# A third buffer for raw and converted weight words, in the place of three attention tiles that are first used from the second batch on

## The chip, the cores and the metric

The kernel runs on one core of a Trainium2 chip. The metric is the time of one launch in device microseconds (us): the median of several runs, 1111.56 us before the change (3 runs, 1110.79 to 1111.98). One further run was taken with the hardware profiler; it took 1109.59 us, and its trace spans 1107.8 us from the first to the last instruction.

## What is computed

Attention with a per-position decay (4 batches, 8 heads, 576 positions, head size 64), then two feed-forward layers over the 2304 tokens that come out of it. The weights arrive as float64.

```
def _attn_ref(q, k, v, f):
    scores = scale * np.matmul(q, k.transpose(0, 1, 3, 2))
    log_f = np.log(np.clip(f, 0.0001, 1.0))
    cum = np.cumsum(log_f, axis=-1)
    decay = cum[:, :, :, None] - cum[:, :, None, :]
    scores = np.where(causal, -1000000000.0, scores + decay)
    attn = softmax(scores)
    return np.matmul(attn, v)

def reference(...):
    x = attn_out as [2304, 512]
    h = x @ moe_w_in                      # 512 -> 2048
    x = np.maximum(0.01 * h, h) @ moe_w_out
    return ((x @ w_a) * (x @ w_b)) @ w_o2  # 512 -> 1536 -> 512
```

## The kernel before, in words

One program interleaves attention and the first feed-forward layer; the second layer follows. A list scheduler decides each engine's order when the program is built, so the order of the source is a priority and not the final order. On the chip every engine then works its own list strictly in order, and so does each queue that issues DMAs (SP issues nearly all of them).

**Attention** is cut into (batch, r): r = 0 is the first 256 queries of a batch, r = 1 the other 320. `att_scores` (L170) makes a head's scores, adds the decay, takes the row's extreme and the exponential; `att_values` (L377) transposes the weights, multiplies them with v and writes its part of a token chunk `xh`, `xl` (a high and a low part whose sum is the f32 value). Batch 0 loads q and k in rows and transposes them on TensorE in f32; from batch 1 on they are transposed on VectorE into tiles `tq` and `tk`, and `qll` holds the low part of q. So `tq`, `tk` and `qll` are first used in batch 1, with one exception: `ones` (L144), at the start, shares the space of `tk`.

**The first layer** works on chunks of 256 tokens: `l1` (L563) multiplies with w_in, 24 matmuls of 128x256 for a pair of feature blocks, `l2` (L591) with w_out. Products take three passes: high by high, low by high, high by low.

**The weights.** 16 blocks of w_in (`wi_0` to `wi_15`) and 16 of w_out (`wo_0` ...) are loaded in the order wi_0, wo_0, wi_1, wo_1, ... by `load_weight` (L105): a DMA of 512 KB brings float64 words into a tile `raw`; ScalarE takes an absolute value of the top words into a tile `c` (L94); VectorE clamps, shifts and merges in four instructions (L95, L96, L97, L100); `split` (L85) then copies the high part on ScalarE (L87) and subtracts on VectorE for the low part (L88, tiles `wi_lo`, `wo_lo`). `raw` and `c` have two buffers each, in the pool `stage`:

```
raw = stg_pool.tile([P, W, 2], I32, tag="raw", bufs=RB, name=f"raw_{name}_{z}")
...
c = stg_pool.tile([P, W], I32, tag="t", bufs=2, name=f"c_{name}_{z}")
```

So the DMA of a block waits until L100 of the block two places ahead of it has read its words. The conversions are interleaved with the attention of batch 0 on VectorE. The main part (after L742) runs `att_steps(0)` with `load_next` every ninth step, then `att_steps(1)` with `load_next` every eighth and a `work` item (an `l1` and the `l2` before it) every sixteenth, then the remaining items of chunk 0, four items of chunk 1, closes `stage` (L769) and goes on with batch 1.

## Time and profile before

| | |
|---|---|
| median of 3 runs | 1111.56 us (1110.79 to 1111.98) |
| the profiled execution's own time | 1109.59 us |
| span of its trace | 1107.8 us |
| TensorE (PE) busy | 97% of the span |
| VectorE (DVE) busy | 55% |
| ScalarE (ACT) busy | 49% |
| GpSimd (POOL) busy | 18% |
| mean traffic of the DMA engines | 78 GB/s |

Busy shares are means over stages that have different limits; the attention of batch 0 with the weights fills the first 166 us or so, and the last 400 us are matmuls almost alone. The granted clock is that of TensorE, 1.00 for 2.4 GHz and 0.50 for 1.2 GHz. Matmuls are pipelined and their ends are modelled in the trace, so how densely they are packed is better read from their starts than from the busy share.

### The profile page before, as it was taken

Reading aid. Unit: us, or ns where it says so; the run is one execution under the profiler, and the core shown is the slowest. Engines: PE = TensorE matmul, PEld = TensorE weight load, DVE = VectorE, ACT = ScalarE, POOL = GpSimd, SP = SyncE. Lnnn points to the kernel's source line nnn. Section 1 sums busy time; section 2 is a strip of 40 time slices with the busy share of each in tenths; the row PEclk is TensorE's granted clock in tenths of the full one; section 3 lists DMA queues with packets and bytes.
Section 4 is the critical chain, followed back from the end, with each engine's and each line's share of the span. In section 5 each row is a group of like instructions: output and inputs, shape, how many; then the busy total and the mean of one; then the engine's idle time right before and its main releaser. Section 6 shows DMA issues by size and latency. Waiting matters only on the chain.

```text
span 1107.8 us, 19615 instructions
## 1 busy us (share of the span) xinstructions
PE 1079.2 (97%) x7021; PEld 967.2 (87%) x7021; DVE 614.0 (55%) x1484; ACT 543.2 (49%) x1257; POOL 204.5 (18%) x434
## 2 busy tenths in 40 slices
PE   5899999999999999999999999999999999999998
PEld 3577779999999999999999997888888888888897
DVE  5869887887777777677478877412111211211122
ACT  4656668878787878768554454312111211211121
POOL 4423322434243432333000000102001000100000
PEclk9879999999999999999999999999999999999999
DMA  7645545442452334422054454202000100100010
GB/s 196 195 130 172 159 120 103 96 94 48 79 124 62 94 58 83 109 62 53 9 165 144 142 152 152 76 1 76 1 1 20 48 1 1 48 1 1 1 39 20
DMA packets 185729, 86.77 MB, mean 78 GB/s; under 512 B 143840, under 2 KB 173536, under 8 KB 185632
## 3 DMA queue, kind: packets, MB, share of 16 engines
q1 hardware_dynamic: 180736, 80.80, 28.6%
q10 hardware_dynamic: 4896, 4.72, 1.3%
q8 instruction: 56, 0.92, 0.4%
q14 instruction: 41, 0.34, 0.1%
HBM read 75.96 MB, written 9.51 MB: 77 GB/s over the span
## 4 chain that ended last, share of the span: by engine, by line
PE 72%; DMA 11%; DVE 8%; ACT 4%; issue 3%; SPq 1%; POOL 0%; ACTq 0%; DVEq 0%; POOLq 0%
PE ab L653 25%; PE o L676 13%; PE h L574 11%; PE y L601 10%; PE s L76 5%; PE av L76 5%; PE pp L76 3%; DMA raw_wa<-in_moe_w_a_dram 3%; DMA raw_wb<-in_moe_w_b_dram 2%; DMA raw_wc<-in_moe_w_out_dram 1%; DMA xq<-in_q_dram 1%; DMA cumb<-cum_dram 1%; DMA raw_wi<-in_moe_w_in_dram 1%; DMA raw_wo<-in_moe_w_out_dram 1%; DMA sy<-y_dram 1%
## 5 line engine op out<-in xcount | busy, mean ns | idle before, releaser
L659 DVE TENSOR_TENSOR p<-ab,p 128x512 f32<-128x512 f32 (+1 forms) x60 | 38.3, 638 | 274.6 <-PE ab L653 272.0
L574 PE MATMUL h<-xh,wi_hi 128*128 128x256 f32 x576 | 164.6, 286 | 1.2 <-ACT wi_hi L87 1.2
L574 PE MATMUL h<-xh,wi_lo 128*128 128x256 f32 x576 | 164.1, 285 | 0.9 <-DVE wi_lo L88 0.9
L574 PE MATMUL h<-xl,wi_hi 128*128 128x256 f32 x576 | 164.3, 285 | 0.0
L601 PE MATMUL y<-gl,wo_hi 128*128 128x256 f32 x576 | 161.7, 282 | 1.0 <-DVE gl L586 1.0
L601 PE MATMUL y<-gh,wo_lo 128*128 128x256 f32 x576 | 161.1, 282 | 0.0
L601 PE MATMUL y<-gh,wo_hi 128*128 128x256 f32 x576 | 159.4, 282 | 0.0
L658 ACT COPY p<-ab 128x512 f32<-128x512 f32 (+1 forms) x60 | 32.7, 544 | 169.1 <-PE ab L653 168.7
L574 PEld LDWEIGHTS h<-xh,wi_hi 128*128 128x128 f32 x576 | 109.8, 191 | 5.2 <-issue 2.3
L574 PEld LDWEIGHTS h<-xh,wi_lo 128*128 128x128 f32 x576 | 109.8, 191 | 2.5 <-DVE wi_lo L88 1.1
L601 PEld LDWEIGHTS y<-gl,wo_hi 128*128 128x128 f32 x576 | 108.4, 188 | 2.9 <-DVE gl L586 1.6
L574 PEld LDWEIGHTS h<-xl,wi_hi 128*128 128x128 f32 x576 | 109.8, 191 | 0.8 <-issue 0.4
L601 PEld LDWEIGHTS y<-gh,wo_lo 128*128 128x128 f32 x576 | 108.3, 188 | 1.7 <-issue 1.2
L601 PEld LDWEIGHTS y<-gh,wo_hi 128*128 128x128 f32 x576 | 107.3, 188 | 1.8 <-issue 0.8
L313 POOL TENSOR_SCALAR p<-cumb,ncum_t 128x384 f32<-128x384 f32 (+1 forms) x112 | 75.1, 678 | 162.4 <-PE pp L76 47.8
L87 ACT CAST pph<-p 128x512 fp32r<-128x512 f32 (+1 forms) x60 | 34.8, 580 | 126.3 <-DVE p L659 126.2
L291 ACT ACTIVATE p<-p,stat 128x384 f32<-128x384 f32 (+4 forms) x128 | 77.0, 603 | 34.5 <-DVE stat L320 27.2
L88 POOL TENSOR_TENSOR yl<-sy,yh 128x512 fp32r<-128x512 f32 (+1 forms) x16 | 19.2, 1211 | 393.7 <-ACT yh L87 393.6
L653 PE MATMUL ab<-yh,wb_hi 128*128 128x512 f32 (+1 forms) x240 | 88.3, 368 | 0.9 <-DVE p L659 0.6
L653 PE MATMUL ab<-yh,wa_hi 128*128 128x512 f32 (+1 forms) x240 | 88.1, 367 | 0.0
L653 PE MATMUL ab<-yh,wa_lo 128*128 128x512 f32 (+1 forms) x240 | 88.1, 367 | 0.0
L653 PE MATMUL ab<-yl,wa_hi 128*128 128x512 f32 (+1 forms) x240 | 88.1, 367 | 0.0
(168 smaller groups left out, 2612.6 us busy)
## 6 DMA issues: line engine op xcount, KB each, us to landing
cumb<-cum_dram SPq DMA_DIRECT2D x32, 288.0 KB, 3.9
raw_wi<-in_moe_w_in_dram SPq DMA_DIRECT2D x16, 512.0 KB, 4.0
raw_wo<-in_moe_w_out_dram SPq DMA_DIRECT2D x16, 512.0 KB, 4.0
raw_wa<-in_moe_w_a_dram SPq DMA_DIRECT2D x12, 512.0 KB, 3.5
raw_wb<-in_moe_w_b_dram SPq DMA_DIRECT2D x12, 512.0 KB, 3.5
raw_wc<-in_moe_w_out_dram SPq DMA_DIRECT2D x12, 512.0 KB, 3.6
xq<-in_q_dram SPq DMA_DIRECT2D x144, 32.0 KB, 2.0
y_dram<-yo ACTq DMA_DIRECT2D x18, 256.0 KB, 3.0
```

Of the source, the lines that this page charges most:

```text
L76: return method(*args, **kw)
L87: nc.scalar.copy(hi, src)
L88: (lo_engine or nc.gpsimd).tensor_tensor(out=lo, in0=src, in1=f32(hi), op=ALU.subtract)
L291: act_att.activation(pt, pt, AF.Exp, bias=stat[:, 0, s : s + 1], scale=-1.0, accum_out=stat[:, 1, s : s + 1])
L313: pool_att.tensor_scalar(pt, cumb[:, :n], 1.0, ncum_t[:, t, bh : bh + 1], op0=ALU.mult, op1=ALU.add)
L574: nc.tensor.matmul(hps[:, u, :], w[:, c * P : c * P + P], x[:, c, :], start=(n == 0), stop=(n == 3 * ND - 1))
L601: nc.tensor.matmul(o, w[:, d * P : d * P + P], g[:, u, :], start=(fi == 0 and n == 0 and d % 2 == 0), stop=(fi == NF1 - 1 and n == 2 and d ...
L653: nc.tensor.matmul(o[:, :tn], w[:, c * P : c * P + P], y[:, c, :tn], start=(m == 0), stop=(m == 3 * ND - 1))
L658: nc.scalar.copy(p[:, :tn], ab[0][:, :tn])
L659: nc.vector.tensor_tensor(out=p[:, :tn], in0=ab[1][:, :tn], in1=p[:, :tn], op=ALU.mult)
L676: nc.tensor.matmul(o, g[:, t * P : t * P + P], w, start=(fi == 0 and m == 0), stop=(fi == NF2 - 1 and m == 2))
```

## The change

Every third weight block (counted by `piece`: wi_1, wo_2, wi_4, wo_5, ..., wo_14, ten in all) takes its `raw` and its `c` from a new pool `more` with one buffer of each, as long as that pool is open. `more` lies in the attention part of the memory. It is closed when `stage` is, before batch 1 of attention, and a new pool `att_b` then takes its place, with `tq`, `qll` (two buffers) and `tk`. `ones` goes to the space of `p4`. Nothing else changes in what is computed.

```
         for z in range(0, 512, W):
-            raw = stg_pool.tile([P, W, 2], I32, tag="raw", bufs=RB, name=f"raw_{name}_{z}")
+            third = "more" in late and piece[0] % 3 == 2
+            piece[0] += 1
+            words, bufs = (late["more"], 1) if third else (stg_pool, RB)
+            raw = words.tile([P, W, 2], I32, tag="raw", bufs=bufs, name=f"raw_{name}_{z}")
...
-            c = stg_pool.tile([P, W], I32, tag="t", bufs=2, name=f"c_{name}_{z}")
+            c = words.tile([P, W], I32, tag="t", bufs=1 if third else 2, name=f"c_{name}_{z}")
...
-    late = {}
+    late, piece = {}, [0]
...
+    more_ctx = att_ctx.enter_context(ExitStack())
+    late["more"] = more_ctx.enter_context(tc.tile_pool(name="more", bufs=1))
...
-    ones = ap_.tile([B * H, S], F32, tag="tk", name="ones")
+    ones = ap_.tile([B * H, S], F32, tag="p4", name="ones")
...
-            tq = ap_.tile([P, 320], F32, tag="tq", name=f"tq_{nm}")
+            tq = late["att"].tile([P, 320], F32, tag="tq", name=f"tq_{nm}")
...
-            qll = ap_.tile([P, 384], F32R, tag="qll", bufs=2, name=f"qll_{nm}")
+            qll = late["att"].tile([P, 384], F32R, tag="qll", bufs=2, name=f"qll_{nm}")
...
-                tk = ap_.tile([P, S], F32, tag="tk", name=f"tk_{nm}")
+                tk = late["att"].tile([P, S], F32, tag="tk", name=f"tk_{nm}")
...
     stage_ctx.close()
+    more_ctx.close()
+    del late["more"]
+    late["att"] = more_ctx.enter_context(tc.tile_pool(name="att_b", bufs=1))
```

The change moves instructions on every engine, since the scheduler sees other waits. (Line numbers in the changed kernel are 3 to 8 higher. In the names, `_0_0_7` is batch 0, r = 0, head 7; the last number is a running one.) Three places:

**SP's queue at the start.** `cumb` are the decay rows for the first heads, `xq` and `xk` queries and keys, `vn` values. Before:

```order
L392 DMA vn_0_0_0_209<-in_v_dram 128x2x64
L392 DMA vn_0_0_2_321<-in_v_dram 128x2x64
L283 DMA cumb_0_0_0_121<-cum_dram_58 128x256 x2
L283 DMA cumb_0_0_2_158<-cum_dram_58 128x256 x2
L194 DMA xq_0_0_4_229<-in_q_dram 128x2x64 x2
L283 DMA cumb_0_0_4_242<-cum_dram_58 128x256
L197 DMA xk_0_0_4_230<-in_k_dram 128x2x64 x2
L283 DMA cumb_0_0_4_242<-cum_dram_58 128x256
L114 DMA raw_wi_1_0_262<-in_moe_w_in_dram 128x4x256
L116 DMA raw_wo_1_0_274<-in_moe_w_out_dram 128x1024
```

With the change:

```order
L397 DMA vn_0_0_0_212<-in_v_dram 128x2x64
L117 DMA raw_wi_1_0_265<-in_moe_w_in_dram 128x4x256
L288 DMA cumb_0_0_0_124<-cum_dram_58 128x256 x2
L288 DMA cumb_0_0_2_161<-cum_dram_58 128x256 x2
L199 DMA xq_0_0_4_232<-in_q_dram 128x2x64 x2
L288 DMA cumb_0_0_4_245<-cum_dram_58 128x256
L202 DMA xk_0_0_4_233<-in_k_dram 128x2x64 x2
L288 DMA cumb_0_0_4_245<-cum_dram_58 128x256
L119 DMA raw_wo_1_0_277<-in_moe_w_out_dram 128x1024
```

The words of wi_1 are now asked for ahead of the decay rows and of the queries and keys of head 4; before they came behind them.

**TensorE (PE) just ahead of the first layer's first matmul** (`h_0_0`; `px` is the transposed output of the last pair of heads of r = 0, the `s`, `s4`, `pp`, `tq`, `tk` rows are attention of r = 1). Before:

```order
L76 MATMUL px_0_0_7_614<-ident_65,xn_0_0_7_587 128x128 x2
L76 MATMUL s4_0_1_0_0_760<-kn_0_1_0_709,qn_0_1_0_708 64x288
L76 MATMUL pp_0_1_0_0_807<-ident_65,p_0_1_0_2_736 128x128 x3
L76 MATMUL s4_0_1_0_1_763<-kn_0_1_0_709,qn_0_1_0_708 64x288
L76 MATMUL pp_0_1_0_1_813<-ident_65,p_0_1_0_3_745 128x128 x4
L76 MATMUL tq_0_1_2_935<-ident_65,xq_0_1_2_925 128x128 x2
L76 MATMUL tq_0_1_2_935<-ident_65,xk_0_1_2_926 128x64
L76 MATMUL tk_0_1_2_0_940<-ident_65,xk_0_1_2_926 128x128 x2
L76 MATMUL s_0_1_1_2_803<-kn_0_1_0_709,qn_0_1_0_708 128x384
L574 MATMUL h_0_0_619<-xh_0_309,wi_0_hi_185 128x256
```

With the change:

```order
L76 MATMUL px_0_0_7_617<-ident_65,xn_0_0_7_590 128x128 x2
L76 MATMUL s_0_1_1_2_806<-kn_0_1_0_712,qn_0_1_0_711 128x384
L76 MATMUL tk_0_1_2_0_943<-ident_65,xk_0_1_2_929 128x128 x2
L76 MATMUL tk_0_1_2_2_947<-ident_65,xk_0_1_2_929 128x128 x2
L76 MATMUL tk_0_1_2_2_947<-ident_65,xk_0_1_2_929 128x64
L76 MATMUL s_0_1_1_3_827<-kn_0_1_0_712,qn_0_1_0_711 128x512
L579 MATMUL h_0_0_622<-xh_0_312,wi_0_hi_188 128x256
```

Four items of r = 1 (`s4` and `pp`, twice each) now stand ahead of `px`, and three more transposes `tk_0_1_2_2` and one more score `s_0_1_1_3` ahead of `h_0_0`. On VectorE the same stretch holds more conversions: of its 160 conversion instructions (L95, L96, L97, L100 and L88 of 32 blocks), 52 stood ahead of the fourth `xl` (the one that reads this `px`), and 71 stand there now: 15, 15, 14, 14 and 13 of the five lines for 11, 11, 10, 10 and 10 before.

**VectorE (DVE) where the conversions end.** Before, words of the last two blocks are converted between instructions of batch 1:

```order
L320 ISA p_1_0_1_1_2265,stat_1_0_0_2176<-s_1_0_1_1_2270,p_1_0_1_1_2265 128x256
L320 ISA stat_1_0_0_2176 128x1
L97 SCALAR_TENSOR_TENSOR c_wo_15_0_1617<-raw_wo_15_0_1615,c_wo_15_0_1617 128x512
L239 STREAM_TRANSPOSE tq_1_0_3_2363<-xq_1_0_3_2358 128x256
L297 RECIPROCAL rec_1_0_0_0_2220<-rec_1_0_0_0_2220 128x2
L270 TENSOR_TENSOR ks_1_0_4_2440<-tk_1_0_4_2438,ks_1_0_4_2440 64x256
L296 TENSOR_SCALAR rec_1_0_1_2_2283<-stat_1_0_0_2176 128x2
L100 SCALAR_TENSOR_TENSOR c_wo_15_0_1617<-raw_wo_15_0_1615,c_wo_15_0_1617 128x512
L297 RECIPROCAL rec_1_0_1_2_2283<-rec_1_0_1_2_2283 128x2
L586 TENSOR_TENSOR gl_0_7_1847<-hs_0_7_1845,gh_0_7_1846 128x512
```

With the change:

```order
L88 TENSOR_TENSOR wo_14_lo_1479<-c_wo_14_0_1482,wo_14_hi_1478 128x512
L96 TENSOR_SCALAR c_wo_15_0_1620<-c_wo_15_0_1620 128x512
L366 ISA p4_0_1_4_1388,stat_0_1_4_1224<-s4_0_1_5_1_1568,p4_0_1_4_1388,st4_0_1_5_1560 64x288
L366 ISA stat_0_1_4_1224 64x1
L244 STREAM_TRANSPOSE tq_1_0_0_2189<-xq_1_0_0_2184 128x256
L268 STREAM_TRANSPOSE tk_1_0_0_2200<-xk_1_0_0_2195 128x256
L88 TENSOR_TENSOR wi_15_lo_1605<-c_wi_15_0_1608,wi_15_hi_1604 128x512
L97 SCALAR_TENSOR_TENSOR c_wo_15_0_1620<-raw_wo_15_0_1618,c_wo_15_0_1620 128x512
```

The first transpose of batch 1, `tq_1_0_0`, follows 156 of the 160 conversion instructions, where it followed 126 before; it cannot stand ahead of those of wo_14, the last block in `more`, whose memory it takes. The last block is now done while heads 5 and 6 of batch 0 are at work.

## Rows read from the trace of the kernel before

**Rows 1.** Busy time, share of the span and instructions of each engine

```profile
PE 1079.2 (97%) x7021; PEld 967.2 (87%) x7021; DVE 614.0 (55%) x1484; ACT 543.2 (49%) x1257; POOL 204.5 (18%) x434
```

**Rows 2.** Stretches: length, busy us (instructions) of each engine, granted clock, DMA share, GB/s

```profile
5.00:10.00 5.00, 2.37 (x13) 1.34 (x11) 2.37 (x6) 2.23 (x6) 0.00 (x0) 1.00 0.98 290
53.60:67.20 13.60, 13.58 (x42) 7.89 (x41) 8.56 (x22) 6.30 (x15) 3.10 (x4) 0.50 0.62 166
69.90:158.00 88.10, 87.26 (x597) 70.22 (x597) 76.97 (x183) 55.20 (x124) 30.53 (x46) 1.00 0.57 158
158.00:162.80 4.80, 2.55 (x20) 2.06 (x18) 4.71 (x17) 2.90 (x8) 0.00 (x0) 1.00 0.18 31
162.80:166.30 3.50, 3.50 (x17) 3.46 (x18) 3.44 (x15) 2.43 (x8) 0.00 (x0) 0.51 0.20 32
166.30:170.00 3.70, 3.70 (x31) 3.46 (x29) 1.94 (x6) 3.65 (x11) 0.00 (x0) 1.00 0.28 46
```

**Rows 3.** Waits of DVE, 0 to 166 us: total us, times, longest

```profile
DVE c_wi L95 <- ACT c_wi L94: 9.7, 9, 2.3
DVE p L320 <- PE s L76: 5.7, 2, 2.9
DVE c_wo L95 <- ACT c_wo L94: 5.2, 5, 2.0
```

**Rows 4.** Waits of DVE, 0 to 58 us

```profile
DVE c_wi L95 <- ACT c_wi L94: 6.3, 6, 2.3
DVE p L76 <- POOL p L76: 2.1, 3, 1.0
...
DVE p L76 <- PE s L76: 1.2, 1, 1.2
DVE c_wo L95 <- ACT c_wo L94: 1.0, 1, 1.0
```

**Rows 5.** Waits of SP's queue, 0 to 166 us

```profile
SPq L116 <- DVE c_wo L100: 28.5, 11, 5.5
SPq L114 <- DVE c_wi L100: 18.0, 10, 2.9
```

**Rows 6.** Timeline of PE, 159.4 to 163.1 us: start, us, what, idle before and its releaser

```profile
159.67 0.27 PE L76 MATMUL s<-ks,qll 128*128 128x128 f32 x1
161.10 0.39 PE L574 MATMUL h<-xh,wi_hi 128*128 128x256 f32 x1 [1.15 <-ACT wi_hi L87]
...
162.76 0.50 PE L574 MATMUL h<-xh,wi_lo 128*128 128x256 f32 x1 [0.92 <-DVE wi_lo L88]
```

**Rows 7.** Groups of DVE by line, 0 to 166 us: busy, mean ns

```profile
L97 DVE SCALAR_TENSOR_TENSOR c_wo<-raw_wo,c_wo 128x512 int32<-128x512 int32 x16 | 12.5, 778 | 0.2
...
L88 DVE TENSOR_TENSOR wi_lo<-c_wi,wi_hi 128x512 fp32r<-128x512 f32 x16 | 11.4, 711 | 0.2
...
L100 DVE SCALAR_TENSOR_TENSOR c_wi<-raw_wi,c_wi 128x512 int32<-128x512 int32 x16 | 11.2, 700 | 0.1
...
L96 DVE TENSOR_SCALAR c_wi<-c_wi 128x512 int32<-128x512 int32 x16 | 7.6, 476 | 0.2
L95 DVE TENSOR_SCALAR c_wo<-c_wo 128x512 f32<-128x512 f32 x16 | 7.5, 466 | 5.2 <-ACT c_wo L94 5.2
```

**Rows 8.** Timeline of DVE, 57.5 to 58.5 us

```profile
57.97 0.41 DVE L76 TENSOR_TENSOR xl<-px,xh 128x256 fp32r<-128x256 f32 x1
```

**Rows 9.** Timeline of PE, 54.9 to 69.9 us

```profile
54.98 0.69 PE L76 MATMUL px<-ident,xn 128*128 128x128 f32 x2
...
60.59 0.69 PE L76 MATMUL tk<-ident,xk 128*128 128x128 f32 x2
61.21 1.65 PE L76 MATMUL s<-kn,qn 64*128 64x384 f32 x2
62.78 0.58 PE L574 MATMUL h<-xh,wi_hi 128*128 128x256 f32 x1
...
67.82 1.12 PE L76 MATMUL s<-kn,qn 64*128 64x512 f32 x2
68.88 0.65 PE L76 MATMUL tk<-ident,xk 128*128 128x128 f32 x3
69.25 0.75 PE L76 MATMUL s<-kn,qn 64*128 64x288 f32 x2
```

**Rows 10.** The chain that ended last, around 190 and 240 us: start, us, what

```profile
189.75 3.59 DMA cumb<-cum_dram
193.51 1.01 POOL p L337
...
239.17 1.07 DVE pl L374 x2
240.29 1.03 PE av L76 x7
```

## The prediction, made before the change was run

> **What bounds the kernel now.** I read first the shares of the whole span [rows 1]: PE is busy for 97%, so a change can save only what PE loses, about 29 us in all plus what it loses to a low clock. Then the stretches [rows 2]. From 69.9 to 158 us, where the weights are still being converted, PE is busy for 87.26 of 88.1 us: it idles 0.84 us there, though the weights are late the whole time. From 158 to 162.8 us it is busy for only 2.55 of 4.80 us, and in the next 3.5 us its granted clock is 0.51, the 1.2 GHz level, with 1.00, 2.4 GHz, on either side. The stretch from 53.6 to 67.2 us also runs at 0.50.
>
> Next the waits. VectorE does wait for weights: 9.7 us before the first instruction of a wi block and 5.2 us before that of a wo block, 14.9 us in all [rows 3]; the releaser named is ScalarE's absolute value, which itself waits for the DMA. SP shows why: the DMAs of weight words waited 28.5 and 18.0 us for L100 to free a buffer [rows 5]. That is the wait which a third buffer loosens. But PE feels little of it: the trace has two waits of PE for a weight in the whole fill, 1.15 us for the high and 0.92 us for the low part of a late w_in block, at 161.10 and 162.76 us [rows 6]. So I price the change by PE's losses, not by VectorE's 14.9 us.
>
> **The change part by part.**
>
> *The end of the fill (a gain).* In the new order the last block is converted while heads 5 and 6 of batch 0 are at work, and no longer between instructions of batch 1. The two waits of PE, 1.15 + 0.92 = 2.07 us [rows 6], should go. What is left of the 2.25 us idle is 0.18 us, for attention. After them PE starts only 17 matmuls in 3.5 us at half clock, against 31 in 3.7 us right behind [rows 2]. Without the hole the clock should stay up, which gives at most half of the stretch, 1.75 us, and at least nothing (if another hole appears); I take 1.5, near the upper end, since PE went into that stretch from 88 us at full clock. Together **-3.6 us**, bounds -3.8 and 0.
>
> *The start (what the front-loading costs).* VectorE works its list in order. Ahead of the fourth `xl`, which completes chunk 0, stand 71 conversion instructions for 52: 4 more of L95, 4 of L96, 4 of L97, 4 of L100, 3 of L88. At 0.47, 0.48, 0.78, 0.70 and 0.71 us [rows 7] that is 4 x 2.43 + 3 x 0.71 = 11.9 us; instructions overlap a little, so say 10 to 11.9. Against this stand VectorE's waits for weights up to 58 us, 6.3 + 1.0 = 7.3 us, which the third buffer can take away, and 2.1 + 1.2 = 3.3 us in which it waited for GpSimd and PE with nothing else to do [rows 4] and where in the new order the conversion of wi_1 stands. So `xl` comes between 10 - 7.3 - 3.3 = 0.6 us earlier and 11.9 - 7.3 = 4.6 us later than the 57.97 us of [rows 8]; I take 1.5 us later, nearer the lower end because those 3.3 us lie exactly where the new work was put. In SP's queue the words of wi_1 move ahead of the first decay rows. The DMA engines are already at 0.98 there and move 290 GB/s [rows 2]; 512 KB at that rate take 1.8 us. That is the upper bound, nothing the lower (the transfers overlap with what nobody waits for yet); I take 0.9. Sum: 2.4 us later on VectorE.
>
> The Trainium skill, "DMA: Bandwidth & Descriptors", section "Issuing engines are not separate DMA queues", says that all DMAs run on the same 16 engines and interleave, whoever issues them. It speaks against asking for weights this early; by it the whole 1.8 us would be paid, and the sum below would be 0.9 us higher.
>
> On PE, `px` (54.98 us) would start at 57.4 us. Behind it now stand `px` itself (0.62 us, by the starts), a score of 384 columns (1.57), two transposes (0.62), three more `tk` (0.37 at full clock, 0.74 at half) and a score of 512 columns (1.06, or 2.12): 5.7 us, so the first `h` starts at 63.1 us for 62.78 us, 0.3 us later. But the last two items, which ran from 67.82 to 69.25 us, 1.43 us of full-clock work, are then already done [rows 9]. Net **-1.1 us**. Bounds: with the lower ends -0.6 - 1.43 = -2.0; with the upper ones 4.6 + 1.8 - 1.43 = +5.0.
>
> *Between 70 and 158 us (nothing, or a little).* PE is packed; its work does not change, and weights that come earlier cannot run on a full engine. The new interleave is another list, and it may hold small holes of its own. The old one cost 0.84 us here; I add the same once more, **+0.8 us**, bounds 0 and 3 (VectorE idles 88.10 - 76.97 = 11.1 us in this stretch, so it has room, but each attention step now queues behind more conversions).
>
> *Edits at no cost.* `ones` in the space of `p4`: it is read once, by the scan at the start, and `p4` is first written in r = 1, long after. `tq`, `tk`, `qll` in `att_b`: the first `tq` has to follow the words of wo_14. Before it stood behind 126 conversions, now behind 156; the cover is that VectorE has lost its 14.9 us of waits by then, which pay for those 30 (30 x 0.63 = 18.9 us) but for 4 us. Should the cover be gone, batch 1 starts 4 us later, the second rival. The last 900 us run the same instructions; PE is simply earlier there.
>
> Sum: -3.6 - 1.1 + 0.8 = **-3.9 us**. Against the profiled execution's own 1109.59 us that is 1105.7 us; that execution was 1.97 us under the median of the runs, so against the median, 1111.56 us, it is **1107.7 us**, 0.35% faster. About 0.2%, 2.2 us, is what a measurement of this kernel can tell from no change.
>
> **The rivals.**
>
> *1. VectorE's bubbles are the bound, and all 14.9 us come off:* 1111.56 - 14.9 = 1096.7 us. For it: VectorE is busy for 76.97 of 88.1 us, and the waits are regular. Against it: PE is packed over the same stretch [rows 2], and a full engine can't follow. Chance 0.05. The Trainium skill, "Perfetto Trace Analysis", section "Optimization Strategy", reads gaps that repeat on the engine that should be saturated as a lack of buffers for the next tile; by it, taken for VectorE, this rival would be the forecast. In this trace the engine that should be saturated is PE, and it has no such gaps.
>
> *2. Batch 1 becomes what PE waits for (no change).* The chain that ended last leaves PE at about 189.75 us, runs over decay rows, GpSimd and VectorE for 50 us and returns to PE at 240.29 us [rows 10]: the attention of batch 1 is just in time now. If PE gets there 4 us earlier and batch 1 does not, PE waits there and the 3.9 us are given back: 1111.6 us. For it: the bound on `tq` above. Against it: with no conversions left VectorE and ScalarE have less between batch 1's steps. That the third buffer frees nothing, since the loads stand in SP's queue behind others, would look the same. Chance 0.22, with the small holes of the new interleave in it.
>
> *3. The start is slower than the end gains (slower).* If VectorE's waits for GpSimd and PE don't absorb anything and the decay rows are late by the full 1.8 us, the first layer starts 5.0 us late net of the work moved ahead. The clock rose only 4.4 us after the first `h` [rows 2, 9], so the half-clock stretch would grow by about the same 5 us, which costs half of that again, 2.5 us. With the gain at the end: +5.0 + 2.5 - 3.6 = +3.9 us, 1115.5 us. It decides from a net delay of about 4 us on. For it: the list in front of the fourth `xl` grew by more than a third. Against it: the 10.6 us of waits that stood there. Chance 0.15.
>
> **How the numbers follow.** The forecast has 0.58. Its own range: from -3.8 - 2.0, and a clock that rises one stretch of 3.5 us earlier in the start (-1.75), which is 7.6 us and 1104.0 us, up to the 0.2% bound, 1109.3 us. Rival 2 holds 1109.3 to 1113.8 us. The range from 1104.0 to 1113.8 us leaves out rivals 1 and 3, 0.20 together. Faster by over 0.2%: 0.58 + 0.05, less 0.02 for a forecast that comes out short, 0.61; within 0.2%: 0.24; slower: 0.15.
>
> **What would show it.** Right: VectorE's waits for ScalarE's absolute value fall from 14.9 us to under 4; PE has no wait for a high or low part of a w_in block after 100 us; no stretch of half clock between 80 and 200 us; the first `h` within 2 us of 62.8 us; and about 4 us less idle and half-clock loss of PE before 170 us. Wrong: a first `h` after 66 us (rival 3); new waits of PE for attention tiles between 166 and 260 us (rival 2); a PE that is not packed from 70 us on but still ends the fill earlier, which would mean that I took modelled ends of matmuls for work (rival 1).

## The result: 0.84% slower, and the profile after

The changed kernel takes 1121.16 us (median of 6 runs) against 1111.77 us for the kernel before in the same session: a ratio of 1.0084 with a 95% interval from 1.0068 to 1.0099, some 9.4 us. I had forecast 1107.7 us, faster. The profiled execution took 1122.02 us, with a span of 1120.1 us for the 1107.8 us of before, 12.3 us more; the profile of before was 2 us under its median, so about 10 us of these are to be explained.

First the shares of the page of the changed kernel, as [rows 1]:

```profile
PE 1087.0 (97%) x7021; PEld 968.6 (86%) x7021; DVE 611.1 (55%) x1484; ACT 542.5 (48%) x1257; POOL 209.3 (19%) x434
```

The instruction counts of all five engines are those of before. So the time lies in when they run. The same stretches as in [rows 2] (length, busy us of each engine, granted clock, DMA share, GB/s):

```profile
53.60:67.20 13.60, 13.60 (x39) 7.37 (x38) 12.01 (x30) 7.14 (x16) 5.54 (x5) 1.00 0.80 216
69.90:158.00 88.10, 88.10 (x591) 71.17 (x591) 70.05 (x171) 52.43 (x117) 30.03 (x41) 1.00 0.49 131
158.00:162.80 4.80, 4.80 (x40) 4.28 (x38) 2.53 (x11) 2.60 (x6) 1.50 (x5) 1.00 0.04 7
162.80:166.30 3.50, 3.50 (x33) 3.50 (x33) 2.58 (x11) 1.81 (x6) 0.13 (x1) 1.00 0.32 72
166.30:170.00 3.70, 3.26 (x25) 2.86 (x25) 1.81 (x9) 3.27 (x12) 0.00 (x0) 1.00 0.28 44
```

The end of the fill did what was forecast: from 158 to 166.3 us PE is busy all the time at 2.4 GHz, where it had lost 2.25 us and run 3.5 us at half clock. In the first stretch VectorE works 12.01 us where it had worked 8.56. (The clock column prints 1.00 there, but the matmuls of `h` start 0.21 us apart up to 72.76 us and 0.117 us behind that, as they had around 67.4 us before: the half-clock stretch ended 5.4 us later.)

Next VectorE's list, with the fourth `xl` for [rows 8], and PE's first `h` for [rows 9]:

```profile
64.91 0.40 DVE L76 TENSOR_TENSOR xl<-px,xh 128x256 fp32r<-128x256 f32 x1
```

```profile
68.58 0.58 PE L579 MATMUL h<-xh,wi_hi 128*128 128x256 f32 x1
```

They are 6.94 and 5.80 us later than before. VectorE's waits from 0 to 166 us, as [rows 3] (total us, times, longest), then those of SP's queue, as [rows 5]:

```profile
DVE p L325 <- PE s L76: 7.1, 5, 2.3
DVE c_wi L95 <- ACT c_wi L94: 6.3, 7, 1.9
DVE p L366 <- PE s L76: 4.9, 3, 3.1
DVE c_wo L95 <- ACT c_wo L94: 4.7, 5, 2.0
```

```profile
SPq L117 <- DVE c_wo L100: 23.0, 9, 8.3
SPq L119 <- DVE c_wi L100: 18.9, 9, 4.5
```

The waits for weights fell only from 14.9 to 11.0 us, those of SP for a free buffer from 46.5 to 41.9. Last the waits of PE from 166 to 360 us, and from 595 to 680 us; before had one of 0.5 us in the first stretch, and 1.0 us for `gl` in the second:

```profile
PE s L76 <- DVE stat L325: 2.9, 2, 1.8
PE h L579 <- ACT hs L589: 1.5, 2, 0.9
PE s L76 <- ACT p L335: 0.7, 1, 0.7
PE s L76 <- DVE st L366: 0.5, 1, 0.5
...
PE y L606 <- DVE gl L591: 3.0, 5, 1.3
PE y L606 <- ACT gh L588: 1.6, 1, 1.6
```

To see where PE falls behind I use a **shift**. Both kernels run the same matmuls, in different orders. I count each with the usual spacing of its shape (0.117 us for an `h` or `y` of 256 columns, 0.226 us for an `ab` of 512) and read from PE's timeline when each kernel has done the same amount of that work. The table gives how much the shift against the profiled execution of before grows in each stretch, in us; the times are those of before, and the last column is the whole shift at 1071 us (what arises behind 668 us has no column of its own).

| kernel | ratio, 95% interval | to 74 | 74-163 | 163-206 | 206-350 | 350-595 | 595-668 | at 1071 |
|---|---|---|---|---|---|---|---|---|
| the change | 1.0084 [1.0068, 1.0099] | +4.3 | -3.5 | -0.1 | +5.5 | +1.0 | +4.6 | +12.3 |
| e1 moved tiles alone | 1.0013 [0.9996, 1.0029] | +1.4 | -0.2 | -0.2 | +2.3 | +0.1 | -0.2 | +3.5 |
| e2 third from piece 24 | 1.0064 [1.0044, 1.0084] | +4.8 | -3.4 | +0.6 | +4.8 | +0.6 | +3.5 | +9.6 |
| e3 third to piece 7 | 1.0082 [1.0064, 1.0101] | +4.4 | -3.3 | -0.7 | +5.2 | +0.8 | +3.7 | +11.0 |
| e4 attention further ahead | 1.0124 [1.0105, 1.0144] | +4.2 | -2.7 | +1.0 | +2.6 | +2.6 | +6.0 | +13.1 |
| e5 third closed at the start | 1.0055 [1.0034, 1.0075] | -0.5 | +3.6 | +1.0 | -0.1 | +1.4 | +2.3 | +7.1 |
| e6 as e5, not from piece 24 | 1.0106 [1.0083, 1.0129] | +1.5 | +3.4 | +1.2 | +6.0 | +0.1 | +3.2 | +15.3 |
| e7 before, lead 290 | 1.0035 [1.0019, 1.0051] | +0.8 | -0.8 | +0.2 | -0.5 | +0.7 | +3.5 | +3.9 |
| e8 before, five pairs first | 1.0041 [1.0022, 1.0061] | -0.3 | -0.9 | -0.3 | +1.1 | +1.9 | +4.5 | +6.0 |
| e9 before, tq behind block 15 | 1.0115 [1.0098, 1.0132] | +1.8 | +0.4 | +0.7 | +5.6 | +1.8 | +6.0 | +14.4 |
| e10 before, tq behind block 13 | 1.0081 [1.0066, 1.0096] | +1.9 | +1.7 | -1.7 | +1.6 | +2.5 | +2.9 | +8.5 |
| e11 as e9, lead 310 | 1.0117 [1.0098, 1.0136] | -1.0 | -1.4 | +1.9 | +6.8 | +2.3 | +4.5 | +13.3 |
| e12 change, low part on GpSimd | 1.0211 [1.0197, 1.0225] | +4.3 | -3.0 | +0.2 | +5.4 | +3.4 | +9.2 | +24.3 |
| e13 before, the same | 1.0150 [1.0133, 1.0167] | +1.9 | +0.2 | +1.2 | -0.2 | +3.0 | +9.6 | +20.4 |
| e14 change, no late clamp | 1.0106 [1.0089, 1.0123] | +4.1 | -2.6 | -0.2 | +5.8 | +0.6 | +6.3 | +13.1 |
| e15 before, the same | 1.0047 [1.0032, 1.0063] | +1.7 | -0.4 | +0.0 | -0.6 | +0.3 | +3.8 | +4.8 |

What one execution is worth can be read from it. Before, e1, e5 to e11, e13 and e15 come to their first `h` by the same list of PE, and at 74 us they scatter from -1.0 to +1.9 us, +0.8 on the mean; the four with the list of the change (the change, e4, e12, e14) stand at +4.1 to +4.3. So the start costs about 3.4 us, and the rest of the 4.3 is luck of the execution that all are measured against. From 206 to 350 us e1, e13 and e15, which keep the order of before, scatter from -0.6 to +2.3 us. The change has four terms that stand out: **+4.3 at the start, -3.5 at the end of the fill, +5.5 in batches 1 to 3 (206 to 350 us), +4.6 from 595 to 668 us**, where the last two chunks of layer 1 run beside the conversion of the second layer's weights. The last stretch holds no line that the diff touches.

### The profile page after: what moved, and what is told of

Same layout as the page of the kernel before. It is cut to its first block, busy times and chain, and to the rows that moved or that the text cites. A ratio compares the mean times of both kernels' runs of the same rounds, so it can differ in the third digit from the quotient of the medians.

```text
span 1120.1 us, 19642 instructions
## 1 busy us (share of the span) xinstructions
PE 1087.0 (97%) x7021; PEld 968.6 (86%) x7021; DVE 611.1 (55%) x1484; ACT 542.5 (48%) x1257; POOL 209.3 (19%) x434
## 4 chain that ended last, share of the span: by engine, by line
PE 74%; DMA 12%; DVE 6%; ACT 3%; issue 2%; SPq 2%; POOL 0%; DVEq 0%; ACTq 0%; POOLq 0%
PE ab L658 23%; PE h L579 12%; PE o L681 12%; PE y L606 11%; PE s L76 6%; PE av L76 5%; PE pp L76 3%; DMA raw_wa<-in_moe_w_a_dram 2%; DMA raw_wb<-in_moe_w_b_dram 2%; DMA cumb<-cum_dram 2%; DMA xq<-in_q_dram 1%; DMA raw_wo<-in_moe_w_out_dram 1%; DMA sy<-y_dram 1%; DMA raw_wc<-in_moe_w_out_dram 1%; SPq L240 1%
## 5 line engine op out<-in xcount | busy, mean ns | idle before, releaser
L318 POOL TENSOR_SCALAR p<-cumb,ncum_t 128x384 f32<-128x384 f32 (+1 forms) x112 | 77.9, 703 | 155.0 <-PE pp L76 70.4
L88 POOL TENSOR_TENSOR yl<-sy,yh 128x512 fp32r<-128x512 f32 (+1 forms) x16 | 19.2, 1210 | 396.7 <-ACT yh L87 396.6
L658 PE MATMUL ab<-yh,wb_lo 128*128 128x512 f32 (+1 forms) x240 | 88.2, 367 | 0.0
```

The lines of the kernel that those rows point to most:

```text
L88: (lo_engine or nc.gpsimd).tensor_tensor(out=lo, in0=src, in1=f32(hi), op=ALU.subtract)
L318: pool_att.tensor_scalar(pt, cumb[:, :n], 1.0, ncum_t[:, t, bh : bh + 1], op0=ALU.mult, op1=ALU.add)
L658: nc.tensor.matmul(o[:, :tn], w[:, c * P : c * P + P], y[:, c, :tn], start=(m == 0), stop=(m == 3 * ND - 1))
```

## The experiments

The theory after this profile (O): the third buffer moves conversions forward in lists that are worked in order, which costs at the start; and since the program's lists are made by a scheduler, it reshuffles everything behind, which costs the rest. The first four runs set it against the moved tiles (M), the start alone (S), the load of the buffer (D) and a late chain of attention (R).

**e1, the moved tiles alone.** No piece uses the third buffer; every list is that of before, row for row.

```diff
-            third = "more" in late and piece[0] % 3 == 2
+            third = False
```

> Only the moved tiles: tq, tk and qll lie in att_b and ones in the space of p4, the pool more is opened and closed but no piece uses it; the lists of PE and VectorE are those of the kernel before, row for row. Theory O (the loss is the new order of the list behind the fill, and the start): no change, 1111.6 us, ratio 0.998 to 1.002, first h at 62.8 us. Theory M (the moved tiles themselves wait for memory): most of the 5.6 us that PE loses in batches 1 to 3 stays, 1115 to 1121 us. Theory S (only the start is to blame): no change.

Measured 1110.73 us against 1109.15, 1.0013 [0.9996, 1.0029]; first `h` at 64.41 us. M is out: `tq`, `tk` and `qll` in `att_b` and `ones` in the space of `p4` cost nothing by themselves.

**e2, the third buffer for two pieces only.**

```diff
-            third = "more" in late and piece[0] % 3 == 2
+            third = "more" in late and piece[0] % 3 == 2 and piece[0] >= 24
```

> The third buffer takes only pieces 26 and 29, so nearly all weights of the start come as before; but from about the 700th of PE's 6875 instructions on, the order is the same as with the full change. Theory O: the shift against before is within 1.5 us at 74 us, then grows as in the full change by 5 to 6 us from 206 to 350 us and by about 5 us from 600 to 720 us; whole 1117 to 1121 us. Theory S: without the late start the loss is gone: 1107 to 1112 us. Theory D (the extra load traffic and conversions cost): two pieces of 32 instead of ten, so a fifth of the loss, 1113 us.

Measured 1116.44 us, 1.0064. From 206 us on it loses what the change loses, +4.8 and +3.5 us, with two pieces instead of ten: D is out. S is not tested by it, since the start is late here too; against S speaks e11 below, which has the start of before (-1.0 us) and loses 6.8 us from 206 to 350 us. The start was missed: +4.8 us where under 1.5 was expected. The free buffer let the scheduler pull the words of a block needed only at the end of the fill (wi_13) ahead, to the 44th place of VectorE's list. Up to 65 us VectorE is busy for only 46.15 us there, but it waits 9.5 us for ScalarE's absolute values, for 6.0 us in e1. Such a wait can be followed to PE: the absolute value of a piece of w_in waits 2.41 us for its words, up to 42.92 us, the attention weights `p` stand behind it in ScalarE's list, and PE idles 3.25 us for them, up to 44.77 us. That a conversion put forward delays PE by its work too is not shown.

**e3, the third buffer for pieces 2 and 5 only.**

```diff
-            third = "more" in late and piece[0] % 3 == 2
+            third = "more" in late and piece[0] % 3 == 2 and piece[0] < 8
```

> The third buffer takes only pieces 2 and 5: the start is that of the full change (the first 79 instructions of VectorE are the same), the rest of the fill runs on two buffers, and the order from about the 730th instruction of PE on is again that of the full change. Theory O: first h at 68 to 69 us and +4 us at 74 us; no or half the gain at the end of the fill; +10 us later: 1120 to 1127 us. Theory S: +4 us at the start and nothing later: 1114 to 1117 us. Theory D: as S, a fifth of the loss later.

Measured 1118.64 us, 1.0082: the change's whole loss with two early pieces; first `h` at 69.89 us. Against O, the gain at the end of the fill came in full (-3.3 us), though all pieces but two had two buffers. The groups of VectorE that make the low part of w_in, from 130 to 166 us (count: shortest, mean, longest ns, first to last), say why; before, e3 and the change:

```profile
L88 DVE TENSOR_TENSOR wi_lo<-c_wi,wi_hi x4: 685/686/770, 132.4 to 162.0; 128x512 fp32r<-128x512 f32 x4
```

```profile
L88 DVE TENSOR_TENSOR wi_lo<-c_wi,wi_hi x3: 673/680/684, 131.7 to 151.6; 128x512 fp32r<-128x512 f32 x3
```

```profile
L88 DVE TENSOR_TENSOR wi_lo<-c_wi,wi_hi x2: 650/668/686, 131.9 to 138.9; 128x512 fp32r<-128x512 f32 x2
```

The last low part is made at 162.0, 151.6 and 138.9 us. Two pieces ahead at the start stay ahead, and 10 us are more than the 2 us that PE had waited.

**e4, attention further ahead from batch 1 on.**

```diff
+    for engine in (pe_att, act_att, dve_att, pool_att):
+        engine.offset = 100
```

> The full change, and from the attention of batch 1 on ScalarE, VectorE, GpSimd and PE put attention 100 instructions further ahead when the order of the list is made. The start and the end of the fill stay (+4.3 and -3.5 us). Theory O, with the loss in batches 1 to 3 because attention stands too late between the matmuls: the 5.6 us from 206 to 350 us fall to under 2 us, whole 1113 to 1118 us. Rival R (it is not where attention stands but that attention's chain started later): the same 5 to 6 us there, 1119 to 1123 us.

Measured 1123.21 us, 1.0124, the wrong way. From 206 to 350 us the loss halves (+2.6 for +5.5), but 350 to 595 us lose 2.6 and the late stretch 6.0. Where attention stands does matter, but a priority moves the loss elsewhere. Neither O nor R is settled by it.

The next four: is the start a matter of conversions in front of attention (O) or of words in flight (T), and are the late losses those of any new order (L)?

**e5, the third buffer closed until chunk 0 is complete.**

```diff
-            third = "more" in late and piece[0] % 3 == 2
+            third = "open" in late and "more" in late and piece[0] % 3 == 2
...
+    gate = late["open"] = late["more"].tile([P, 512, 2], I32, tag="raw", bufs=1, name="gate")
+    nc.vector.tensor_copy(f32(gate[:, 0:2, 0]), f32(xl[0][:, HP - 1, 0:2]))
```

> The third buffer is closed until the fourth xl of chunk 0 is written (one copy of 128x2 on VectorE after it), and then used for the rest of the fill; VectorE's first 118 instructions and PE's first 215 are those of the kernel before. Theory O (at the start the third buffer puts conversions, whose words have not landed, in front of attention in the lists of ScalarE and VectorE): first h at 62.5 to 65 us for 68.6, shift against the run of the moved tiles alone within 1 us at 74 us, the gain of 1 to 3 us at the end of the fill kept, 5 to 9 us lost after it; whole 1113 to 1117 us. Rival T (the start is late because more words travel at once and attention's rows come later): the same, since fewer travel. Rival M (memory or semaphores of the moved tiles): first h stays at 67 us or later, whole 1119 to 1122 us.

Measured 1117.14 us, 1.0055; first `h` at 63.26 us and the shift at 74 us -0.5. The start is restored; O and T are both content with that. PE's own list up to the first `h` is that of before here as well, so the run does not tell what the conversions do from what PE's order does. But a loss came back 30 us later, and this time its mechanism can be seen. ScalarE's timeline of e5 (start, us, what, idle before and its releaser), then PE's:

```profile
94.69 0.48 ACT L432 COPY ph<-pp 128x384 f32<-128x384 f32 x1
101.31 0.66 ACT L94 ACTIVATE c_wo<-raw_wo 128x512 f32<-128x512 f32 x1 [6.15 <-DMA raw_wo<-in_moe_w_out_dram]
101.88 0.57 ACT L432 COPY ph<-pp 128x512 f32<-128x512 f32 x1
```

```profile
102.50 0.69 PE L76 MATMUL tk<-ident,xk 128*128 128x128 f32 x2 [4.51 <-ACT ph L432]
```

The absolute value of a piece waits 6.15 us for its words at the head of ScalarE's list. Behind it stands the copy of `ph` for attention, which needs nothing from that DMA, and PE idles 4.51 us for the copy. A conversion whose buffer is free but whose words are not there holds up all that is behind it.

**e6, as e5, and two buffers for the last eight pieces.** The condition of e5 with `and piece[0] < 24`.

> As the closed start, and the third buffer also not for pieces 24 to 31, so that the last words have two buffers and the first tq of batch 1 stands at row 256 of VectorE's list, for 288, while the last conversion stands at 329, for 309 (before: 247 and 341). Theory O (the hole at the end of the fill comes and goes with the order in which batch 1 and the last conversions stand, not with the buffer): the hole is partly back, half of the 3.3 us. Theory B (only a third buffer at the end closes the hole): all of the hole is back, PE waits 2 us for wi_hi and wi_lo. After the fill 4 to 9 us are lost as before under O; whole 1113 to 1119 us.

Measured 1123.19 us, 1.0106. PE has no wait for wi_hi or wi_lo here either, though the last low part of w_in comes at 163.01 us, as late as before: PE was itself 4.8 us late by then, 3.5 us of it in a wait of the kind of e5. So the run does not tell O from B, as I had thought it would.

**e7 and e8, new orders without any third buffer.** First the lead of attention in the scheduler's priorities, then one pair more of chunk 1 ahead of batch 1.

```diff
-            self.engine, self.offset = engine, 300
+            self.engine, self.offset = engine, 290
```

> The kernel before, without any third buffer or moved tile; one number of the list maker is changed, the lead of attention in priority, 290 for 300. PE's first 2020 instructions (to about 305 us) and VectorE's first 712 stay in order, the rest is shuffled by a few places. Theory L (the kernel before had a good order behind 305 us by luck, and any shuffle loses): no shift until 300 us, then +3 to +8 us, most of it from 600 to 670 us; whole 1114 to 1119 us. Rival (the late loss has to do with the third buffer): no change, 1110 to 1113 us.

```diff
-    for item in one[:4]:
+    for item in one[:5]:
...
-    for item in one[4:]:
+    for item in one[5:]:
```

> The kernel before, without any third buffer or moved tile; one pair of blocks of chunk 1 more is written ahead of batch 1's attention in the program (five for four). The first 317 instructions of VectorE and 640 of PE are as before, so the fill with its hole stays; the last 3562 instructions of PE are in the order of the full change. Theory L: start and hole as before (shift within 1.5 us up to 166 us), 2 to 4 us lost from 200 to 350 us and 3 to 5 us from 600 to 670 us; whole 1115 to 1119 us. Rival (the loss has to do with the third buffer): no change, 1110 to 1113 us.

Measured 1113.95 us, 1.0035 [1.0019, 1.0051], and 1115.84 us, 1.0041 [1.0022, 1.0061], both slower than before. e7 is level with before up to 595 us and loses 3.5 us from there to 668 us. e8, whose order there is that of the change, instruction for instruction on PE and VectorE, loses 4.5 us, and the change 4.6. L holds for the late stretch, without a third buffer or a moved tile. It does not hold for 206 to 350 us: e8 has an order of its own there and loses 1.1 us.

The stretch from 600 to 670 us of e1, which has the order of before, of the change, and of e7:

```profile
600.00:670.00 70.00, 69.08 (x559) 67.28 (x559) 55.90 (x100) 34.33 (x62) 0.00 (x0) 1.00 0.49 151
```

```profile
600.00:670.00 70.00, 65.36 (x544) 63.71 (x543) 55.20 (x99) 33.84 (x61) 0.00 (x0) 1.00 0.47 140
```

```profile
600.00:670.00 70.00, 66.81 (x530) 63.94 (x529) 53.25 (x97) 34.65 (x63) 0.00 (x0) 1.00 0.47 144
```

VectorE and ScalarE do the same work, to 2.7 us, and PE loses 0.9, 4.6 and 3.2 us.

**e9, e10 and e11, is it the buffer or the order that closes the hole at the end of the fill?** Two buffers, no moved tile; the first `tq` of batch 1 waits for the last conversion (e9), for that of block 13 (e10, with 13 for 15 in the edit), and e9 with a lead of 310 (e11).

```diff
+    hold = ap_.tile([P, 320], F32, tag="tq", name="hold")
+    nc.vector.tensor_copy(hold[:, 0:2], f32(wa[15][3][:, 0:2]))
     att_tail(0)
     for _ in att_steps(2):
```

> The kernel before with two buffers and no moved tile; one copy of 128x2 on VectorE makes the first tq of batch 1 wait for the last conversion of the fill (block 15). VectorE's first 253 and PE's first 515 instructions are as before; the last conversion stands at row 316 (before 341), the first tq right behind it (before 247). Theory O (the hole at 158 to 166 us is the order of batch 1 and the last conversions, not the lack of a buffer): no wait of PE for wi_hi or wi_lo, about -3 us at 166 us against before; then 1 to 5 us lost in batches 1 to 3 and 4 us from 600 to 670 us; whole 1111 to 1117 us. Theory B (a third buffer is needed): the hole stays, 2 us of waits.

> As the run before, but the first tq of batch 1 waits for block 13 only: the words of blocks 14 and 15 are still converted between instructions of batch 1, the last at row 341 as in the kernel before. Theory O: the hole stays or is up to half closed (shift 0 to -2 us at 166 us), 4 us lost from 600 to 670 us; whole 1113 to 1118 us. Theory B: the hole stays whole.

> As the first run of these three, and attention's lead in the list maker is 310 for 300: the same order up to the 3114th instruction of PE (some 455 us), another one behind it. Theory L (what is lost from 600 to 670 us is drawn anew by each order, and hardly any order is as good as the old one): 2 to 6 us lost there, whole 1109 to 1117 us. A loss under 1 us there would give 1107 to 1109 us, a kernel faster than both.

Measured 1122.14, 1118.16 and 1122.26 us: 1.0115, 1.0081, 1.0117. The named waits for weights shrink (0.5 us in e9), but the shift gains nothing: +0.4, +1.7 and -1.4 us from 74 to 163 us. The low part of w_in in e9:

```profile
L88 DVE TENSOR_TENSOR wi_lo<-c_wi,wi_hi x4: 678/690/692, 133.5 to 162.5; 128x512 fp32r<-128x512 f32 x4
```

With batch 1 out of the way the last low part is still made at 162.5 us, and the hole only came earlier: from 150 to 158 us PE is busy for 6.72 of 8.00 us. In e10 it is made at 166.2 us, in e11, which has the order of e9 here, at 158.6; the change has it at 138.9, e3 at 151.6. So the order alone does not bring the words that far forward, and O falls as the whole cause. B fits better: no run without a third buffer gained more than 1.4 us (e11). But e3 has two buffers at the end, so it is enough to have used the third one early.

**e12 and e13, VectorE relieved in the late stretch with GpSimd's help.** The low part of the second layer's weights is made by GpSimd, which is idle there; on the change, and on the kernel before.

```diff
-            split(hi[:, z : z + W], lo[:, z : z + W], from_double(raw, c), nc.vector)
+            split(hi[:, z : z + W], lo[:, z : z + W], from_double(raw, c), None if "wx" in pools else nc.vector)
```

> The full change; in the late stage (weights of the second layer, L626 to L631) the low part of a weight is made by GpSimd, which is idle there, and no longer by VectorE: 0.69 us of the 2.9 us of VectorE per piece go. The order up to PE's 4764th instruction (some 590 us) is that of the full change. Theory V (gl and gh stand behind conversions in the lists of VectorE and ScalarE, and PE has under 1 us of slack for them): the 5 us lost from 600 to 670 us fall to 1 to 3 us, whole 1117 to 1120 us. Rival W (the loss there is the words' landing, whatever engine converts): 4.5 to 6 us lost as before, 1121 us. Rival C (a slower low part, 1.2 us on GpSimd, keeps words' buffers and weights later): over 6 us lost, 1122 to 1126 us.

> The same single edit on the kernel before. Theory V: from 600 to 670 us before loses some 2 us in three waits of PE; 0 to 2 us of them go, whole 1109.5 to 1112 us, and no loss of 4 us although the late order is a new one. Theory L (any new order loses there): +3 to +5 us, 1114 to 1117 us. Rival C: over +3 us as well, with waits of PE for low parts of wa, wb or wc.

Measured 1133.53 and 1127.88 us, 1.0211 and 1.0150: far more than any theory had said. C alone has the sign in e12, but its mechanism is not there: PE has no wait for a low part of wa, wb or wc up to 760 us, in either run. VectorE did not get free. Of its groups from 595 to 720 us, and of PE's waits from 595 to 760 us, in e12:

```profile
L97 DVE SCALAR_TENSOR_TENSOR c_wb<-raw_wb,c_wb 128x512 int32<-128x512 int32 x10 | 13.1, 1307 | 0.2
```

```profile
PE y L606 <- DVE gl L591: 8.8, 9, 1.8
```

In the change L97 takes 688 ns there. VectorE has 23 instructions fewer from 600 to 670 us, and is busy for 55.75 us, as long as before (55.20). PE's waits for `gl` go from 3.0 to 8.8 us.

**e14 and e15, VectorE relieved without GpSimd.** Without L95 for the second layer's weights.

```diff
-        nc.vector.tensor_scalar(t, t, TOP_MIN, TOP_MAX, op0=ALU.max, op1=ALU.min)
+        if "wx" not in pools:
+            nc.vector.tensor_scalar(t, t, TOP_MIN, TOP_MAX, op0=ALU.max, op1=ALU.min)
```

> The full change; the clamp of L95 is left out for the weights of the second layer (L626 to L631): 0.43 us of VectorE's 2.9 us per piece go, 30 times, and nothing goes to GpSimd. The order up to PE's 4451st instruction is that of the full change. Theory V (VectorE's list is what keeps gl from PE): of the 5 us lost from 600 to 670 us 2 to 4 go, 1117 to 1119 us. Rival W (the words' landing or ScalarE's list alone): 4 to 6 us stay lost, 1120 to 1123 us.

> The kernel before with the same clamp left out. Theory V: 0 to 2 us gained from 600 to 670 us, 1108 to 1111 us, though the late order is a new one. Theory L (any new order loses there): 3 to 5 us lost, 1113 to 1116 us.

Measured 1121.83 and 1114.49 us, 1.0106 and 1.0047. VectorE is busy for 51.30 us from 600 to 670 us in e14, for 55.20, and PE loses 6.3 us there for 4.6. The kernel before, relieved in the same way, loses 3.8 us. V falls as a matter of VectorE's load: less of it gains nothing. W had the time of e14 right (1120 to 1123 us), and L fits all runs; the two do not exclude each other. On unchanged work four orders of the late stretch were run: the old one (before and e1) loses nothing; that of the change, which e2, e3, e5, e6, e8, e9 and e10 share on PE and ScalarE, 2.3 to 6.0 us; that of e7 and e11 3.5 and 4.5; that of e4 6.0. e14 and e15 share one more, and lose 6.3 and 3.8. So one and the same order varies by 2 to 4 us from run to run, and that the old one loses nothing rests on two executions.

How such an order costs time can be seen at 614 us in the change. ScalarE, VectorE and PE:

```profile
613.19 0.67 ACT L94 ACTIVATE c_wa<-raw_wa 128x512 f32<-128x512 f32 x1 [2.52 <-DVE c_wc L100]
613.76 0.59 ACT L588 ACTIVATE gh<-h 128x512 fp32r<-128x512 f32 x1
614.24 0.62 ACT L87 CAST wc_hi<-c_wc 128x512 fp32r<-128x512 f32 x1
614.75 0.60 ACT L589 ACTIVATE hs<-h 128x512 f32<-128x512 f32 x1
```

```profile
615.42 0.68 DVE L88 TENSOR_TENSOR wc_lo<-c_wc,wc_hi 128x512 fp32r<-128x512 f32 x1
616.02 0.69 DVE L591 TENSOR_TENSOR gl<-hs,gh 128x512 fp32r<-128x512 f32 x1
```

```profile
609.60 0.28 PE L606 MATMUL y<-gh,wo_hi 128*128 128x256 f32 x1
...
616.76 0.39 PE L606 MATMUL y<-gl,wo_hi 128*128 128x256 f32 x1 [0.80 <-DVE gl L591]
```

The `h` that this `gh` reads was complete when PE turned to the `y` of 609.60 us. From there PE runs 24 matmuls of that `y` and 24 of the next `h`, and comes at 615.68 us to the `y` that needs `gl`: 6.1 us, and `gh`, `hs` and `gl` take 0.59 + 0.60 + 0.69 = 1.9 us. The time went on ScalarE. The absolute value of a piece of w_a stood at the head of its list and waited 2.52 us, by the profile for VectorE's L100 of the piece before; `gh`, which needs nothing from it, started only behind it, at 613.76 us. This is the kind of wait seen in e5. Then one cast of 0.62 us between `gh` and `hs`, and one `lo` ahead of `gl`, are enough for PE to wait 0.80 us. In e1 a `gh` stands behind such an absolute value too (it waited 1.86 us for words, up to 614.15 us), but there `gl` is done at 616.53 us and PE comes to it at 616.73. In the old order such places are fewer: PE's waits for `gl` there sum to 0.9 us in e1.

No version tried is faster than the kernel before. What sets the better orders apart from 206 to 350 us stays open: the change, e2, e3, e12 and e14 have the same order there and lose 4.8 to 5.8 us each, e9 and e11 share another and lose 5.6 and 6.8, e5 and e8 have orders of their own and lose -0.1 and 1.1 us. The start of batch 1 alone does not decide it: the first transpose of batch 1 comes at 138.2 us in the change, 131.3 before, and at 151.3 us in e5.

## Why the prediction was wrong

**The end of the fill: right.** -3.6 us forecast, -3.5 measured from 74 to 163 us (-3.0 and -2.6 in e12 and e14, which have the same fill), with the two waits and the half-clock stretch gone as described. Some 0.8 us of it are PE's idle time of before ahead of 158 us [rows 2], which the forecast did not count as a gain. That it is the buffer that does it is the better supported reading (e3, e9 to e11), with no run that isolates it.

**The start: wrong in sign.** -1.1 forecast, between -2.0 and +5.0; +4.3 measured (4.1 to 4.3 in four executions), some 3.4 against the mean of those with the start of before. What failed is the sum on PE: "On PE, `px` (54.98 us) would start at 57.4 us", and with 5.7 us behind it "the first `h` starts at 63.1 us for 62.78 us, 0.3 us later". It gave `px` only VectorE's delay, and left out the work that the new order puts ahead of it, the four items of `s4` and `pp` and the `tq`. In the change:

```profile
58.43 1.22 PE L76 MATMUL s<-kn,qn 64*64 64x288 f32 x2
...
63.33 0.69 PE L76 MATMUL px<-ident,xn 128*128 128x128 f32 x2
```

They take 63.33 - 58.43 = 4.90 us, and from `px` to the first `h` it is 5.25 us. That makes 10.15 us of work without a gap, where before needed 7.80 us from `px` to `h`. So the `tk` and `s` items put ahead of `h` cost 2.35 us at half clock, against the 1.43 us that they take at full clock where they stood before, and the first `h` could not have come before 65.1 us, with nothing late at all.

From 52.40 us on VectorE's list, by which I had priced the start, decides nothing: PE has no idle time from there to the first `h`, and ScalarE's cast of this `px`, on which `xl` depends, waits for PE:

```profile
64.06 0.37 ACT L76 CAST xh<-px 128x256 fp32r<-128x256 f32 x1 [0.18 <-PE px L76]
```

The 5.80 us by which the first `h` came later (less 1.43 they are the +4.3 of the table) have two more parts. PE started the twelve `av` and the scores of 384 columns ahead of this work 1.23 us later (52.40 us for 51.17); the decay rows and the conversions put forward can have a part in that. And it needed 6.03 us for them, for 3.81 before: 2.22 us, which are luck of the execution of before. Of the same list, before and e1:

```profile
51.17 1.55 PE L76 MATMUL av<-vn,ph 128*128 128x64 f32 x12 [0.87 <-DVE xl L76]
```

```profile
50.66 2.83 PE L76 MATMUL av<-vn,ph 128*128 128x64 f32 x12 [0.89 <-DVE xl L76]
```

Before, e5, e8 and e11 do the twelve in 1.55 to 1.71 us, the spacing of full clock, and have their first `h` at 62.65 to 63.26 us; e1, e6, e7, e9, e10, e13 and e15 take 2.8 us, at half clock, and have it at 64.41 to 65.37. The change takes 2.82 us too, and so do e4, e12 and e14, with the first `h` at 67.98 to 68.59. Like against like it is some 3.3 us late, of which 2.35 are the work put ahead. Why the clock differs there is open.

The step on VectorE failed as well: "Against this stand VectorE's waits for weights up to 58 us, 6.3 + 1.0 = 7.3 us, which the third buffer can take away"; both ends of my bound took all 7.3 off. Up to 65 us VectorE is busy for 52.46 us, against 46.61 before and 44.98 in e1, and its waits of the change from 0 to 65 us are:

```profile
DVE c_wi L95 <- ACT c_wi L94: 3.1, 4, 1.0
DVE c_wo L95 <- ACT c_wo L94: 2.2, 3, 1.3
...
DVE p L76 <- PE s L76: 1.2, 2, 0.8
...
DVE p L76 <- POOL p L76: 0.8, 2, 0.6
```

Of 7.3 us 5.3 are left, of 3.3 us 2.0. By this sum `xl` would come 11.9 - 2.0 - 1.3 = 8.6 us later; it came 6.9 us later, but because `px` did. The waits did not go with the buffer: up to 65 us those of SP for a free buffer fell from 11.0 to 6.6 us, while ScalarE waited 9.4 + 6.2 = 15.6 us for the DMA of words, for 8.3 + 2.9 = 11.2 us before. I had taken VectorE's waits for waits for a buffer.

The decay rows were the smaller part: GpSimd's wait for them grew from 11.2 to 12.4 us (11.7 in e1). The Trainium skill, "DMA: Bandwidth & Descriptors", section "Issuing engines are not separate DMA queues", says that all DMAs interleave on the same engines; that the whole 1.8 us would be paid was my reading of it, and this trace shows 0.7 to 1.2.

**From 70 to 158 us: nothing lost, the lower bound.** PE is busy for all 88.10 us; I had added 0.8.

**"The last 900 us run the same instructions; PE is simply earlier there": wrong, and the larger error.** The instructions are the same, their order is not. From 163 us on the change loses 5.5 + 1.0 + 4.6 us. e1 shows that the tiles have no part in it, e2 that two pieces in the third buffer are enough for it, e7 and e8 that for the late part no third buffer is needed; e9 and e11 lose 5.6 and 6.8 us from 206 to 350 us without one as well, in an order of their own. The step took the lists behind the fill for unchanged because the lines are.

**The rivals.** Rival 1 is out: the time went up while the waits fell by 3.9 us. By the rule of the Trainium skill, "Perfetto Trace Analysis", section "Optimization Strategy", it would have been the forecast had one taken VectorE for the engine to be saturated; this trace speaks against it. Rival 2 named the right place, new waits of PE for attention behind 166 us, but held that PE could only give back what it had gained; it lost 2 us more than that. Rival 3 has the sign of the start (a first `h` after 66 us), but not its cause, since it put the delay on VectorE's waits and the decay rows. And start and end together come to +0.8 us at 163 us, not +3.9: the clock rose 4.2 us after the first `h`, for 4.6 before, so the half clock did not add half of the delay once more.

## What to carry over

Where lists are worked in order and made by a scheduler, one more buffer is a change of all the lists: follow the order to the end of the program, and time a neutral reorder (a priority changed by 3%, as in e7) as a control before a gain or a loss is put down to the buffer. A wait is worth what its cause is: more buffers take away a wait for a buffer, and leave or lengthen one for words that have not landed, so look at what the engine ahead (here ScalarE) waits for. And price an instruction that starts early by what stands behind it: when an order changes, add up everything that now stands ahead of the instruction whose start you forecast, at the clock that it will run at.

## What the runs showed of the hardware

With GpSimd working beside it, VectorE's instructions got longer: L97 from 688 to 1307 ns for `c_wb` (884 and 916 for the other two), L100 from 686 to 883 ns for `c_wa`, each with two inputs from SBUF; GpSimd took 1.34 to 1.41 us for a low part that takes VectorE 0.69. A quarter of VectorE's conversions moved away left its busy time where it was. The Trainium skill, "GPSIMD Engine Reference", section "1. Specifications", says that GpSimd shares its SBUF interfaces with VectorE and contends with instructions that have two SBUF inputs or run in a 2-port perf mode. The trace agrees on the first. L95, with one input, went up too for `c_wc`, from 426 to 669 ns; whether it runs in such a mode no run here shows.
